# Earlier k and q loads, a step's shift of the value products, and VectorE's work re-dealt, in a kernel of attention and two MLPs

## The chip, the core and the metric

The kernel runs on one core of a Trainium2 chip. The metric is the device time of one execution in microseconds, as the median of several runs. TensorE does the matrix products, ScalarE (ACT) the activations, VectorE (DVE) the elementwise work; GpSimd (POOL) and SyncE (SP) mainly issue DMAs here, each into a DMA queue of its own.

## What is computed

```python
# attention: 4 batches, 12 heads, 448 positions, head size 64
scores = cap * tanh((q @ k^T / sqrt(64)) / cap)
attn   = softmax(scores)
x      = (attn @ v) as 1792 x 768
# first MLP: 768 -> 2048 -> 768
h = relu(x @ w_in);  x = (h * h) @ w_out
# second MLP: 768 -> 2048 -> 768
h = x @ w_in2;       out = (h * sigmoid(1.702 * h)) @ w_out2
```

## The kernel before

Attention comes first, the two MLPs after it. The MLPs' products are formed in Strassen's manner from seven products of sums; every fp32 operand is split into a rounded part and a rest (three matmuls for one product). The weights arrive in a form that has to be unpacked: a **chunk** of weights is loaded raw (`wraw`, on POOL's queue), ScalarE and VectorE unpack it (`join`: one `sx` on ACT, one `wy` on DVE), VectorE forms sums (`sums`: four operations), and POOL writes the result to DRAM scratch (`wsa`, `wsb`), from where SP loads it again for the products. There are 17 chunks for the first MLP; 11 of them are unpacked during attention, the rest in the first MLP's first phase.

Attention runs over 24 pairs of heads, two at a time: 12 **quads** of 4 heads. Each quad has four **steps** c = 0 to 3, one for each chunk of key positions; step s of the whole is 4n + c for quad n, and c = 3 is called TAIL. In a step TensorE makes the scores of both pairs (`sps`), ACT does tanh from PSUM and then exp, and TensorE multiplies earlier exponentials with `ones` (`vsps`, the softmax sums) and with v (`vxps`, `vyps`), as the table `PV` says: an entry (m, part, at) is for the quad m before the present one, its part s, x or y, and its key chunk. `take` copies the three sums out of PSUM, `invert` takes the reciprocal (DVE), `divide` multiplies and writes to DRAM scratch `xs` over POOL's queue; the entries (c, d) of `INVERT` and `DIVIDE` say in which step, and for the quad d before.

k and q of a pair are loaded by SP (`load_pair`), transposed on TensorE through the identity (`kps`, `qps`, or into the free half of a score bank, named `sps`), and split by DVE (`prep_k`, `prep_q`). A pair's k lies in one of two buffers `kz[p % 2]`, q in one of two of the pool `ld`. The steps in which they are transposed are not touched by the change: for quad m, pair 0's k in step 4m - 5, its q in step 4m - 4, pair 1's k and q in step 4m - 1. SP's queue is strictly in order: a load that waits for its buffer holds back all behind it.

`x_slice` (table `X_AT`) reads pieces of `xs` back and forms the first MLP's operands (`form`, and differences `sub`), three slices of five steps each: a read, then four times ACT and DVE work.

In each engine the instructions keep the order in which the program is written (`in_order`); `later` and `flush` put some DVE work at the next step's start. The loop over s at the end of the function issues attention, loads, weight slots (`ATT_WORK`, one `join` or `sums` each) and slices.

Of the kernel before, what the change touches and what calls it, by code (L numbers as in the profile page):

```python
# [677 lines left out]
def bounded_cap(ctx, tc, q, k, v, cap, w1, w2, w3, w4, out, over):  # L678

    nc = tc.nc  # L680
# [19 lines left out]
    Q_RAW = nc.gpsimd  # L700
# [9 lines left out]
    xf_p = att.enter_context(tc.tile_pool(name="xf", bufs=3, side="right"))  # L710
# [5 lines left out]
    ld = early.enter_context(tc.tile_pool(name="ld", bufs=2, side="right"))  # L716
# [25 lines left out]
    kz = [kz_p.tile([P, NCH, 2, D], F32, name=f"kz{i}") for i in range(2)]  # L742
# [33 lines left out]
    def load_pair(b, p):  # L776

        kt = kz[p % 2]
        qt = ld.tile([CP, NCH, 2, D], F32, tag="q", name="qt")
        queue = nc.scalar if (b, p) in quads[0] else Q_LOAD  # L780
        for j in range(2):
            Q_LOAD.dma_start(out=kt[:, :TAIL, j], in_=k[b, 2 * p + j, :MAIN].rearrange("(p c) d -> p c d", c=TAIL))
        for j, r in halves():
            Q_LOAD.dma_start(out=kt[r, TAIL, j], in_=k[b, 2 * p + j, MAIN:])
        for j in range(2):
            queue.dma_start(out=qt[:, :, j], in_=q[b, 2 * p + j].rearrange("(p c) d -> p c d", c=NCH))
        raw[b, p] = (qt, kt)
# [19 lines left out]
    def prep_k(b, p, ps=None):  # L807
        if ps is None:
            ps = transposed(raw[b, p][1], "kps")
        kk = prep[b, p, "k"] = qk_p.tile([P, 2, KW], F32R, tag="kk", name="kk")  # L810
        if (b, p) in quads[0]:
            a_.activation(kk[:, 0, :], ps, AF.Copy)
        else:
            v_.tensor_copy(kk[:, 0, :], ps)
        v_.tensor_tensor(kk[:, 1, :], ps, f32(kk[:, 0, :]), ALU.subtract)  # L815

    def prep_q(b, p, ps=None):
        if ps is None:
            ps = transposed(raw[b, p][0], "qps")
# [22 lines left out]
    def tanhs(b, p, c):  # L842
        if c == TAIL:
            e = et[b, p, c] = e_p.tile([P, 1, S], F32, tag="et", name="e", bufs=3)
# [27 lines left out]
    def take(n):  # L872

        last = wide("xo") if n == len(quads) - 1 else None
        for i, ps in enumerate(pvp[n]):
            t = x_p.tile([P, S], F32, tag=f"x{i}", name=f"x{i}") if last is None else last[:, i]
# [17 lines left out]
    def start_pair(b, p):  # L894
        prep_q(b, p, transposed(raw[b, p][0], "qps", ps_m.tile([P, 512], F32, tag="m", name="qps")))
        prep_k(b, p)

    def attn_step(s):
        n, c = divmod(s, NCH)
        ahead = quads[n + 1 : n + 3]  # L900
        for f, (at, d) in ((invert, INVERT), (divide, DIVIDE)):
            if c == at and 0 <= n - d < len(quads):
                f(n - d)
        now = quads[n] if n < len(quads) else ()
        more = []
        for i, x in enumerate(now):
# [3 lines left out]
            if c == TAIL and ahead:  # L910

                t = raw[ahead[0][1]][1 - i]
                more.append(transposed(t, "qps" if i else "kps", sc[(*x, c)][:, 1]))
# [6 lines left out]
        if c == TAIL and len(ahead) > 1:  # L920
            raw[ahead[1][0]] += (transposed(raw[ahead[1][0]][1], "kps"),)
# [5 lines left out]
        if c == 2 and 0 < n <= len(quads):  # L927
# [3 lines left out]
        if c == TAIL and len(ahead) > 1:  # L931
            prep_k(*ahead[1][0], raw[ahead[1][0]][2])

    def attn_loads(s):

        for d, f, i in ((6, load_pair, 0), (4, load_pair, 1), (1, load_v, 0), (0, load_v, 1)):
            m, at = divmod(s + d, NCH)
            if at == 0 and m < len(quads) and (m or f is load_v):
# [3 lines left out]
    def chunk_steps(l, kind, i):  # L942
# [77 lines left out]

    def weight_group(m):
# [11 lines left out]
    def weight_slot():  # L1033

        busy = False
        while work and (not busy or work[0][0].__name__.startswith("load")):
            f, *a = work.pop(0)
            if f.__name__ == "join":
# [112 lines left out]
    def x_slice(i, step):  # L1151
# [3 lines left out]
        def get(name, b, k0):  # L1155
            t = xin[name] = xf_p.tile([P, S], F32, tag=name, name="x" + name, bufs=1)
            Q_PUT.dma_start(out=t, in_=xs[b, k0 + i])

        def form(s, name):
# [4 lines left out]
            x = xin[name]  # L1164
# [3 lines left out]
        def sub(o, x, y):  # L1168
            o, x, y = xin[o], xin[x], xin[y]
# [227 lines left out]
    nc.gpsimd.memset(kz[1][:, TAIL], 0.0)  # L1397
    nc.scalar.dma_start(out=capt, in_=cap.rearrange("(o n) -> o n", o=1).to_broadcast([P, 1]))
    for x in quads[0]:
        load_pair(*x)  # L1400
# [4 lines left out]
    for s in range(-2, NCH * len(quads) + 3):  # L1405
        flush()
        if s >= 0:
            attn_step(s)
        attn_loads(s)
        flush()  # L1410
        if s == W_FIRST:
            weight_group(ATT_CHUNKS)
# [3 lines left out]
        if s in X_AT:  # L1416
            x_slice(*divmod(X_AT.index(s), 5))
# [75 lines left out]
E_BUFS = 10  # L1493
# [17 lines left out]
W_AT = 14  # L1511
W_AHEAD = 4
A_WORK = {(0, 0): 6, (0, 1): 6, (1, 0): 7}
# [46 lines left out]
```

## Time and profile before

| | |
|---|---|
| median of 3 runs | 1124.72 us (1120.51 to 1126.14) |
| the profiled execution's own time | 1117.81 us |
| its span, first to last instruction | 1116.0 us |
| TensorE busy in the span | 1053.9 us (94%) |
| VectorE, ScalarE, GpSimd busy | 826.2, 685.9, 278.6 us |
| moved by DMA | 228.36 MB |

The profiled execution lies 0.6% under the median of the runs. TensorE is busy for 94% of the span, so what it waits for, and the clock at which it runs, are read first.

### The profile page before, as it was taken

The numbers are of one execution on the slowest core, as the hardware profiler recorded it, in microseconds if no ns is written. First come the engines' busy times: TensorE is split into PE (matmuls) and PEld (weight loads), VectorE is DVE, ScalarE is ACT, GpSimd is POOL, SyncE is SP. The second block draws the span as 40 slices with busy tenths as digits, with TensorE's granted clock in tenths as the row PEclk, the third lists the DMA queues.
The fourth block names the chain that finished last, engine by engine and source line by source line (L and its number), as shares of the span: only waits on it lengthen the run. The fifth ranks groups of instructions, "written<-read, shape, count | busy, mean of one in ns | idle before, by whom it ended". The sixth has DMA issues, their size and how long they took to land.

```text
span 1116.0 us, 17045 instructions
## 1 busy us (share of the span) xinstructions
PE 1053.9 (94%) x5887; PEld 868.7 (78%) x5887; DVE 826.2 (74%) x1156; ACT 685.9 (61%) x1072; POOL 278.6 (25%) x418
## 2 busy tenths in 40 slices
PE   4998979799899999999999999999999999999997
PEld 2544434346799999989999998999799879998996
DVE  2487769768577987877689869778995885569854
ACT  2897868695567656466675655667555455565551
POOL 1042334321353013113210322343021520000133
PEclk9998989899999999999999999999999999999999
DMA  6399889854798467678864776898443743333433
GB/s 169 87 263 287 245 238 271 260 159 155 214 349 301 150 224 258 210 250 294 309 228 153 267 260 186 283 310 279 140 148 101 223 135 108 106 116 107 149 106 86
DMA packets 149616, 228.36 MB, mean 205 GB/s; under 512 B 65600, under 2 KB 102592, under 8 KB 149520
## 3 DMA queue, kind: packets, MB, share of 16 engines
q0 software_dynamic: 36768, 122.32, 33.9%
q1 hardware_dynamic: 110512, 104.29, 31.2%
q8 instruction: 48, 0.79, 0.3%
q10 hardware_dynamic: 2240, 0.57, 0.3%
q14 instruction: 48, 0.39, 0.1%
HBM read 166.53 MB, written 60.56 MB: 203 GB/s over the span
## 4 chain that ended last, share of the span: by engine, by line
PE 67%; DMA 10%; issue 9%; DVE 8%; ACT 3%; POOL 2%; SPq 0%; DVEq 0%; ACTq 0%; POOLq 0%
PE pa L1138 30%; PE pb L1138 28%; PE sps L834 3%; DMA kz<-in_k_dram 3%; DMA qt<-in_q_dram 3%; DVE form L1147 3%; DVE wl L1115 2%; DMA vz<-in_v_dram 2%; PE vxps L867 2%; PE vsps L867 2%; PE vyps L867 1%; DMA wf<-wsa 1%; ACT form L1146 1%; POOL wsb L994 1%; DVE qu L1348 1%
## 5 line engine op out<-in xcount | busy, mean ns | idle before, releaser
L1138 PE MATMUL pa<-form,wh 128*128 128x448 f32 x1536 | 441.0, 368 | 6.0 <-DVE form L1147 4.9
L1138 PE MATMUL pb<-form,wh 128*128 128x448 f32 x1152 | 330.3, 368 | 3.2 <-ACT qu L1345 2.3
L1138 PEld LDWEIGHTS pa<-form,wh 128*128 128x128 f32 x1536 | 288.9, 188 | 34.5 <-DVE form L1147 6.3
L1138 PE MATMUL pa<-form,wl 128*128 128x448 f32 x768 | 283.0, 368 | 4.9 <-DVE wl L1115 4.8
L1114 ACT ACTIVATE wh<-wf 128x384 fp32r<-128x384 f32 (+1 forms) x392 | 211.2, 560 | 75.8 <-DMA wf<-wsa 28.0
L1115 DVE TENSOR_TENSOR wl<-wf,wh 128x384 fp32r<-128x384 f32 (+1 forms) x392 | 225.9, 607 | 27.5 <-ACT wh L1114 27.0
L1138 PEld LDWEIGHTS pb<-form,wh 128*128 128x128 f32 x1152 | 217.2, 189 | 23.9 <-ACT qu L1345 3.1
L1138 PE MATMUL pb<-form,wl 128*128 128x448 f32 x576 | 211.4, 367 | 0.0
L1138 PEld LDWEIGHTS pa<-form,wl 128*128 128x128 f32 x768 | 144.8, 189 | 20.4 <-DVE wl L1115 7.8
L1328 POOL DMA_DIRECT2D out_dram<-o x92 | 57.7, 634 | 252.3 <-DVE o L1326 248.3
L1138 PEld LDWEIGHTS pb<-form,wl 128*128 128x128 f32 x576 | 108.4, 188 | 9.5
L1147 DVE TENSOR_TENSOR form<-g,form 128x1344 fp32r<-128x1344 f32 (+1 forms) x72 | 100.7, 1399 | 9.4 <-ACT form L1146 8.7
L847 ACT ACTIVATE e<-sps 128x896 f32<-128x896 f32 (+1 forms) x96 | 75.7, 822 | 47.7 <-PE sps L834 41.9
L979 DVE SCALAR_TENSOR_TENSOR wy<-wraw,sx 128x768 int32<-128x768 int32 (+1 forms) x68 | 61.8, 908 | 46.1 <-ACT sx L975 46.1
L1345 ACT ACTIVATE qu<-pb 128x448 f32<-128x448 f32 x88 | 47.5, 540 | 67.2 <-PE pb L1138 67.1
L834 PE MATMUL sps<-qq,kk 64*128 64x448 f32 (+1 forms) x504 | 81.0, 405 | 7.8 <-DVE kk L815 2.4
L1146 ACT ACTIVATE form<-g 128x1344 fp32r<-128x1344 f32 (+1 forms) x72 | 85.8, 1191 | 2.0 <-DVE g L1302 1.9
L834 PEld LDWEIGHTS sps<-qq,kk 64*128 64x128 f32 (+1 forms) x504 | 52.6, 198 | 43.5 <-ACT e L851 19.0
L851 ACT ACTIVATE e<-e,ecap 128x896 f32<-128x896 f32 (+1 forms) x96 | 85.7, 947 | 0.0
L975 ACT ACTIVATE sx<-wraw 128x768 f16<-128x768 bf16 (+1 forms) x68 | 69.5, 1022 | 0.0
L963 POOL DMA_DIRECT2D wraw<-in_moe_w_out_dram x72 | 53.2, 743 | 49.5 <-DVE wy L979 24.4
L1348 DVE SCALAR_TENSOR_TENSOR g<-pa,qu 128x448 f32<-128x448 f32 x64 | 39.8, 621 | 31.6 <-ACT qu L1345 16.8
(111 smaller groups left out, 1016.6 us busy)
## 6 DMA issues: line engine op xcount, KB each, us to landing
wf<-wsa SPq DMA_DIRECT2D x224, 192.0 KB, 4.0
wf<-wsb SPq DMA_DIRECT2D x168, 256.0 KB, 3.2
wraw<-in_moe_w_in_dram POOLq DMA_DIRECT2D x32, 766.5 KB, 8.3
wraw<-in_moe_w_out_dram POOLq DMA_DIRECT2D x48, 383.2 KB, 6.5
wsa<-wy POOLq DMA_DIRECT2D x32, 384.0 KB, 5.1
wsb<-wy POOLq DMA_DIRECT2D x24, 384.0 KB, 4.9
wsa<-ws POOLq DMA_DIRECT2D x16, 384.0 KB, 5.7
wraw<-in_moe_w_out_dram POOLq DMA_DIRECT2D x24, 255.5 KB, 5.6
```

The lines of the kernel that those rows point to most:

```text
L834: nc.tensor.matmul(ps[:, u, :S], x, y, start=all(t[0] != u for t in todo[:n]), stop=all(t[0] != u for t in todo[n + 1 :]),)
L847: a_.activation(e, chunk(c, sc.pop((b, p, c)))[:, :, :S], AF.Tanh)
L851: a_.activation(e, e, AF.Exp, scale=ecap)
L867: nc.tensor.matmul(ps[32 * i : 32 * i + 32, :S], x, t, start=c == 0, stop=c == TAIL, skip_group_check=True,)
L975: a_.activation(z, words(BF16)[:, :, :, 2], AF.Copy)
L979: v_.scalar_tensor_tensor(y[:, : 2 * n].bitcast(I32), words(I32)[:, :, :, 0], 13, sx[:, : 2 * n], ALU.logical_shift_right, ALU.bitwise_or,)
L1114: a_.activation(x, src, AF.Copy)
L1115: later.append(lambda: v_.tensor_tensor(y, src, f32(x), ALU.subtract))
L1138: nc.tensor.matmul(ps[:, :S], a[:, kk % 4, :], r, start=(s in (1, 5) and kk == 0 and n == 0), stop=(kk == ks - 1 and n == 2), skip_group_c ...
L1146: a_.activation(f[:, 0, :n, :], src, AF.Copy)
L1147: later.append(lambda: v_.tensor_tensor(f[:, 1, :n, :], src, f32(f[:, 0, :n, :]), ALU.subtract))
L1328: nc.gpsimd.dma_start(out=out[b * S : (b + 1) * S, m * P + 32 * j : m * P + 32 * j + 32].rearrange("(c p) d -> p c d", p=32), in_=o[32 * j ...
```

## The change

- k and q are loaded by functions of their own. k has four buffers (`KB`), by the pair's index, and q three (`QB`). `LOADS` requests pair 0's k in step 4m - 10 and its q in 4m - 8, pair 1's k in 4m - 8 and its q in 4m - 7 (before: pair 0 in 4m - 6, pair 1 in 4m - 4), and both pairs' v in 4m - 1 (before: 4m - 1 and 4m). The loop begins at s = -6 so that the first requests are made.
- Products with v are one step sooner (`PV`), and so are `take` and the last reads of the exponentials; these have 8 and 2 buffers, before 10 and 3.
- The reciprocal moves to c = 2, the division to c = 0; weight slots are at TAIL, and two at c = 0; the x slices lie in steps 25 to 48 (before 27 to 44), with two buffers each.
- Ten chunks are unpacked in attention and seven in the first MLP, whose slots begin at its 10th product (before: the 14th). The eleventh chunk is a small one (two thirds of the others).
- Before the first raw weights are loaded, POOL copies one element of a TAIL exponential of quad 0 into `ones` and restores it.
- `raw_queue`, `held`, `RAW_AT` stay without effect while `RAWQ` is POOL's queue.

```diff
-    kz = [... for i in range(2)]
+    kz = [... for i in range(KB)]
...
-    def load_pair(b, p):
-        kt = kz[p % 2]
-        qt = ld.tile([CP, NCH, 2, D], F32, tag="q", name="qt")
...
+    def load_k(b, p):
+        kt = raw[b, p, "k"] = kz[pairs.index((b, p)) % KB]
...
+    def load_q(b, p):
+        qt = raw[b, p, "q"] = ld.tile([CP, NCH, 2, D], F32, tag="q", name="qt")
...
-        for d, f, i in ((6, load_pair, 0), (4, load_pair, 1), (1, load_v, 0), (0, load_v, 1)):
+        for d, f, i in LOADS:
+            f = {"k": load_k, "q": load_q, "v": load_v}[f]
             m, at = divmod(s + d, NCH)
...
         if s == W_FIRST:
+            nc.gpsimd.tensor_copy(ones[:1, 0, :1], et[(*pairs[0], TAIL)][:1, 0, :1])
+            nc.gpsimd.memset(ones[:1, 0, :1], 1.0)
             weight_group(ATT_CHUNKS)
...
-E_BUFS = 10
+E_BUFS = 8
 PV = (
-    ((1, 1, 0), (1, 2, 0), (1, 1, 1)),
     ((1, 2, 1), (1, 0, 2), (1, 1, 2)),
     ((1, 2, 2), (1, 0, 3), (1, 1, 3), (1, 2, 3)),
     ((0, 0, 0), (0, 0, 1)),
+    ((0, 1, 0), (0, 2, 0), (0, 1, 1)),
 )
-INVERT = (0, 2)
-DIVIDE = (1, 2)
-ATT_CHUNKS = 11
+TAKE = 1
+INVERT = (2, 1)
+DIVIDE = (0, 2)
+ATT_CHUNKS = 10
-ATT_WORK = tuple(sorted([4 * n + i for n in range(1, 11) for i in (3, 5, 6)] + [12, 20, 28]))
-X_AT = tuple(s + 6 * i for i in range(3) for s in (27, 29, 30, 31, 32))
+ATT_WORK = tuple(sorted([4 * n + i for n in range(1, 11) for i in (3, 4, 4)]))
+X_AT = (25, 27, 29, 31, 33, 29, 35, 37, 39, 41, 36, 43, 45, 47, 48)
-W_AT = 14
+W_AT = 10
+LOADS = ((8, "q", 0), (8, "k", 1), (7, "q", 1), (10, "k", 0), (1, "v", 0), (1, "v", 1))
+KB = 4
+QB = 3
-A_WORK = {(0, 0): 6, (0, 1): 6, (1, 0): 7}
+A_WORK = {(0, 0): 17 - ATT_CHUNKS, (0, 1): 6, (1, 0): 7}
```

On SP, in the first quads, the queue of before is this (`kz_115`, `kz_116` are the k buffers, `vz` the v buffers):

```order
L782 DMA kz_115<-in_k_dram 128x3x64 x2
L784 DMA kz_115<-in_k_dram 64x64 x2
L786 DMA qt<-in_q_dram 112x4x64 x2
L792 DMA vz_117<-in_v_dram 128x2x192
L797 DMA vz_117<-in_v_dram 64x64 x2
L782 DMA kz_116<-in_k_dram 128x3x64 x2
L784 DMA kz_116<-in_k_dram 64x64 x2
L786 DMA qt<-in_q_dram 112x4x64 x2
L792 DMA vz_118<-in_v_dram 128x2x192
L797 DMA vz_118<-in_v_dram 64x64 x2
```

and of the change, from the first v load on, this:

```order
L792 DMA vz_119<-in_v_dram 128x2x192
L797 DMA vz_119<-in_v_dram 64x64 x2
L792 DMA vz_120<-in_v_dram 128x2x192
L797 DMA vz_120<-in_v_dram 64x64 x2
L787 DMA qt<-in_q_dram 112x4x64 x2
L779 DMA kz_116<-in_k_dram 128x3x64 x2
L781 DMA kz_116<-in_k_dram 64x64 x2
L787 DMA qt<-in_q_dram 112x4x64 x2
L779 DMA kz_117<-in_k_dram 128x3x64 x2
L781 DMA kz_117<-in_k_dram 64x64 x2
```

The number of loads is the same; a k load now goes into a buffer that was last read two quads earlier, and both v loads of a quad stand together, ahead of the q and k of the quad after the next.

On TensorE, around TAIL of quad 1, the program of before has this:

```order
L834 MATMUL sps<-qq,kk 128x448 x3
L804 MATMUL sps<-ident,kz_116 128x128 x4
L834 MATMUL sps<-qq,kk 128x448 x3
L804 MATMUL sps<-ident,qt 128x112 x4
L804 MATMUL kps<-ident,kz_115 128x128 x4
L867 MATMUL vsps<-e,ones 32x448 x8
L834 MATMUL sps<-qq,kk 128x448 x12
```

and that of the change this:

```order
L867 MATMUL vsps<-e,ones 32x448 x8
L834 MATMUL sps<-qq,kk 128x448 x3
L804 MATMUL sps<-ident,kz_116 128x128 x4
L834 MATMUL sps<-qq,kk 128x448 x3
L804 MATMUL sps<-ident,qt 128x112 x4
L804 MATMUL kps<-ident,kz_117 128x128 x4
L867 MATMUL vxps<-e,vz_121 32x448 x2
L867 MATMUL vxps<-e,vz_122 32x448 x2
L867 MATMUL vyps<-e,vz_121 32x448 x2
L867 MATMUL vyps<-e,vz_122 32x448 x2
L867 MATMUL vxps<-e,vz_121 32x448 x2
L867 MATMUL vxps<-e,vz_122 32x448 x2
```

The softmax sums (`vsps`) moved ahead of TAIL's scores, and three groups with v fill the place between the transposes and the next quad's scores (`sps` x12, which follow). Each row `x2` is twice that many matmuls in the profile.

On POOL, before the first raw weights, the change has two instructions that wait for attention, where before the loads followed the memsets at once:

```order
L1411 MEMSET vz_121 128x128
L1411 MEMSET vz_122 128x128
L1426 COPY ones<-e 1x1
L1427 MEMSET ones 1x1
L964 DMA wraw<-in_moe_w_in_dram 128x6x1022 x3
```

So the three raw loads come after quad 0's TAIL exponential and after the `vsps` of step 4 on TensorE.

## Rows read from the trace of the kernel before

**Rows 1.** Waits of TensorE from 0 to 300 us: total us, times, longest us.

```profile
PE qps L804 <- DMA qt<-in_q_dram: 16.3, 3, 6.7
PE kps L804 <- DMA kz<-in_k_dram: 15.6, 3, 6.3
PE sps L834 <- DVE kk L815: 2.4, 2, 1.4
PE sps L834 <- DVE qq L822: 2.1, 5, 0.4
```

**Rows 2.** Busy time by stretch: three quads, quads 0 to 11, first MLP.

```profile
core 0: us, PE busy (x) PEld busy (x) DVE busy (x) ACT busy (x) POOL busy (x), PEclk, DMA share, GB/s
51.52:68.55 17.03, 17.03 (x156) 8.58 (x155) 13.25 (x18) 15.16 (x20) 4.37 (x6) 1.00 0.76 184
68.55:86.25 17.70, 17.29 (x156) 8.53 (x155) 15.36 (x22) 16.40 (x21) 7.43 (x12) 1.00 1.04 309
86.25:109.28 23.03, 17.88 (x156) 8.83 (x155) 16.23 (x23) 17.59 (x23) 7.41 (x10) 0.91 0.97 284
...
34.49:252.93 218.44, 194.81 (x1676) 94.53 (x1675) 158.41 (x221) 171.78 (x223) 69.00 (x97) 0.95 0.81 231
...
300.00:450.00 150.00, 150.00 (x739) 138.71 (x740) 124.12 (x178) 100.11 (x164) 44.13 (x64) 1.00 0.77 255
```

**Rows 3.** TensorE in order of time: start us, us, instruction, idle before.

```profile
8.57 1.49 PE L834 MATMUL sps<-qq,kk 64*128 64x448 f32 x6 [0.69 <-ACT kk L812]
16.71 1.01 PE L804 MATMUL qps<-ident,qt 112*128 112x112 f32 x4 [6.66 <-DMA qt<-in_q_dram]
...
30.46 1.49 PE L834 MATMUL sps<-qq,kk 128*128 128x448 f32 x3 [1.80 <-ACT e L847]
...
51.52 1.71 PE L867 MATMUL vsps<-e,ones 128*32 128x448 f32 x16
...
85.71 0.60 PE L804 MATMUL kps<-ident,kz 128*128 128x128 f32 x4
...
108.26 1.09 PE L804 MATMUL kps<-ident,kz 128*128 128x128 f32 x4 [5.15 <-DMA kz<-in_k_dram]
109.28 2.98 PE L867 MATMUL vsps<-e,ones 128*32 128x448 f32 x16
...
199.75 0.57 PE L804 MATMUL qps<-ident,qt 112*128 112x112 f32 x4 [3.55 <-DMA qt<-in_q_dram]
```

**Rows 4.** Busy time by stretch, columns as in Rows 2, behind a wait.

```profile
110.00:111.00 1.00, 1.00 (x12) 0.40 (x8) 0.97 (x3) 0.00 (x0) 0.00 (x0) 0.50 1.04 279
```

**Rows 5.** The chain that ended last: start us, us, what; two loads.

```profile
4.76 11.90 DMA qt<-in_q_dram
...
97.00 11.16 DMA kz<-in_k_dram
```

**Rows 6.** DMA queues from 0 to 20 us: packets, MB, share of 16 engines.

```profile
q0 software_dynamic: 528, 2.35, 38.5%
```

**Rows 7.** The page's DMA issues: count, KB each, median us to landing.

```profile
wraw<-in_moe_w_in_dram POOLq DMA_DIRECT2D x32, 766.5 KB, 8.3
...
wsa<-wy POOLq DMA_DIRECT2D x32, 384.0 KB, 5.1
...
qt<-in_q_dram SPq DMA_DIRECT2D x44, 112.0 KB, 5.4
```

**Rows 8.** DMA queues from 68 to 217 us (q0 POOL's, q1 SP's).

```profile
q0 software_dynamic: 9451, 29.21, 60.5%
q1 hardware_dynamic: 32488, 9.65, 29.8%
```

**Rows 9.** SP's DMA queue from 127 to 152 us.

```profile
q1 hardware_dynamic: 3789, 1.12, 20.0%
```

**Rows 10.** Transfers that write or read `xs`.

```profile
DMA to landing us min/median/max: 4.9/7.9/11.4
```

**Rows 11.** Transfers from `xs` into `xt`.

```profile
DMA to landing us min/median/max: 6.6/8.7/9.8
```

More of the change, by code (lines that the diff above doesn't have):

```diff
@@ L784, in load_pair @@
             Q_LOAD.dma_start(out=kt[r, TAIL, j], in_=k[b, 2 * p + j, MAIN:])
+    def load_q(b, p):
+        qt = raw[b, p, "q"] = ld.tile([CP, NCH, 2, D], F32, tag="q", name="qt")
+        queue = nc.scalar if (b, p) in quads[0] else Q_LOAD
         for j in range(2):
             queue.dma_start(out=qt[:, :, j], in_=q[b, 2 * p + j].rearrange("(p c) d -> p c d", c=NCH))
-        raw[b, p] = (qt, kt)
     def load_v(b, p):
@@ L808, in prep_k @@
         if ps is None:
-            ps = transposed(raw[b, p][1], "kps")
+            ps = transposed(raw[b, p, "k"], "kps")
         kk = prep[b, p, "k"] = qk_p.tile([P, 2, KW], F32R, tag="kk", name="kk")
@@ L818, in prep_q @@
         if ps is None:
-            ps = transposed(raw[b, p][0], "qps")
+            ps = transposed(raw[b, p, "q"], "qps")
         qq = prep[b, p, "q"] = qk_p.tile([P, 2, S], F32R, tag="qq", name="qq")
@@ L875, in take @@
         for i, ps in enumerate(pvp[n]):
-            t = x_p.tile([P, S], F32, tag=f"x{i}", name=f"x{i}") if last is None else last[:, i]
+            t = x_p.tile([P, S], F32, tag=f"x{i}", name=f"x{i}", bufs=2 if i else 1) if last is None else last[:, i]
             if i:
@@ L894, in start_pair @@
     def start_pair(b, p):
-        prep_q(b, p, transposed(raw[b, p][0], "qps", ps_m.tile([P, 512], F32, tag="m", name="qps")))
+        prep_q(b, p, transposed(raw[b, p, "q"], "qps", ps_m.tile([P, 512], F32, tag="m", name="qps")))
         prep_k(b, p)
@@ L901, in attn_step @@
         for f, (at, d) in ((invert, INVERT), (divide, DIVIDE)):
-            if c == at and 0 <= n - d < len(quads):
+            if c == at and 0 <= n - d < len(quads) - 1:
                 f(n - d)
@@ L910, in attn_step @@
             if c == TAIL and ahead:
-                t = raw[ahead[0][1]][1 - i]
+                t = raw[(*ahead[0][1], "q" if i else "k")]
                 more.append(transposed(t, "qps" if i else "kps", sc[(*x, c)][:, 1]))
@@ L920, in attn_step @@
         if c == TAIL and len(ahead) > 1:
-            raw[ahead[1][0]] += (transposed(raw[ahead[1][0]][1], "kps"),)
+            kps = transposed(raw[(*ahead[1][0], "k")], "kps")
         for m, part, at in PV[c]:
@@ L926, in attn_step @@
             exps(*x, c)
-        if c == 2 and 0 < n <= len(quads):
+        if c == TAKE and 0 < n <= len(quads):
             take(n - 1)
@@ L931, in attn_step @@
         if c == TAIL and len(ahead) > 1:
-            prep_k(*ahead[1][0], raw[ahead[1][0]][2])
+            prep_k(*ahead[1][0], kps)
     def attn_loads(s):
-        for d, f, i in ((6, load_pair, 0), (4, load_pair, 1), (1, load_v, 0), (0, load_v, 1)):
+        for d, f, i in LOADS:
+            f = {"k": load_k, "q": load_q, "v": load_v}[f]
             m, at = divmod(s + d, NCH)
-            if at == 0 and m < len(quads) and (m or f is load_v):
+            if at == 0 and 0 <= m < len(quads) and (m or f == load_v):
                 f(*quads[m][i])
@@ L1019, in bounded_cap @@
     work = []
+    raw_queue = [RAWQ(nc)]
+    held = []
     def weight_group(m):
@@ L1037, in weight_slot @@
             f, *a = work.pop(0)
-            if f.__name__ == "join":
+            if f.__name__ == "load" and raw_queue[0] is nc.sync:
+                held.append((step_now[0] + 2, f, a))
+            elif f.__name__ == "join":
                 f(*a)
@@ L1396, in bounded_cap @@
     nc.vector.memset(kz[0][:, TAIL], 0.0)
-    nc.gpsimd.memset(kz[1][:, TAIL], 0.0)
+    for t in kz[1:]:
+        nc.gpsimd.memset(t[:, TAIL], 0.0)
     nc.scalar.dma_start(out=capt, in_=cap.rearrange("(o n) -> o n", o=1).to_broadcast([P, 1]))
     for x in quads[0]:
-        load_pair(*x)
+        load_k(*x)
+        load_q(*x)
     emit_const()
@@ L1404, in bounded_cap @@
     start_pair(*pairs[0])
-    for s in range(-2, NCH * len(quads) + 3):
+    step_now = [0]
+    for s in range(-6, NCH * len(quads) + 3):
         flush()
+        step_now[0] = s
         if s >= 0:
```

29 lines of the change are left out of this document (17 added, 12 removed).

## The prediction

> **What bounds the kernel now.** I read the busy times by stretch first [rows 2]. In 150 us of the first MLP TensorE has no idle time (150.00 us busy), so next to nothing is to be had there, except by disturbing it. In attention it is different. A quad without waits at full clock takes 17.03 us, all of it TensorE. From the `vsps` of quad 0 to those of quad 11 eleven such spans would be 11 x 17.03 = 187.3 us; the trace has 218.4, that is 31.1 us more. Next the waits [rows 1]: TensorE stood 15.6 us for k and 16.3 us for q. Of the three waits for q one lies between the quads (3.55 us) and two at the start: the second pair's (6.66 us [rows 3]) and the first q's, the remaining 6.1 us, before which nothing can run. So 15.6 + 3.6 = 19.2 us lie between the quads. Another 4.5 us are waits for VectorE's `kk` and `qq`. The rest, 31.1 - 19.2 - 4.5 = 7.4 us, is slow clock: behind a wait the same 16 `vsps` take 2.98 us instead of 1.71 [rows 3], and the granted clock there is 0.50, the 1.2 GHz level, although TensorE is at work again for the whole stretch [rows 4]. So late loads cost 26.6 us between the quads.
>
> Why they are late: the chain shows one k load issued at 97.00 that took 11.16 us [rows 5]; TensorE needed it at 103.1 and got it at 108.2, with 5.15 us of wait [rows 3]. Its buffer had been free since the transposes at 85.71 [rows 3], the TAIL before, but SP's queue, in order, came to it only at 97. With 21 us of lead the 11 us would not hurt.
>
> VectorE and ACT are next in line: in a quad of 17.70 us, 17.29 of them TensorE's, they were busy 15.36 and 16.40 us [rows 2]. So TensorE stays the floor at 17.03, but by 0.6 us over ACT.
>
> **The change, part by part.** Gains are counted against the profiled execution's own 1117.81 us.
>
> *Start.* The second pair's q took 11.90 us [rows 5], while POOL's raw weight loads moved 2.35 MB of the first 20 us, 38.5% of all engines' time, 7.7 us [rows 6]. The change holds them until step 4. The first pair's scores end at 8.57 + 1.49 = 10.1 [rows 3], so the wait of 6.66 us can vanish. Against that, more k and q of quad 1 may be issued at once, about 670 KB: at 217 GB/s (below) up to 3 us. **+6.0** (3.6 to 6.6). The gate itself: POOL's two tiny writes stand between the `vsps` of steps 4 and 5, where TensorE has 12 score matmuls and more to do; nothing. The loads then fall into quads 0 and 1, still before their first `join` in step 7.
>
> *k and q between the quads.* With four and three buffers the tightest load is pair 0's q: its buffer is read last in step 4m - 9, it is needed in 4m - 4, five steps or 21 us. Pair 0's k is asked for in 4m - 10 and needed in 4m - 5, pair 1's k and q get six steps or more. v is needed one step sooner (4m + 3) and is asked for in 4m - 1, its buffers free in 4m - 3: four steps, 17 us, and nothing else is queued ahead of it that waits longer than it does. All exceed the 11 to 12 us of the slowest two loads in the chain [rows 5]. SP issues as many loads as before. **+26.6** if no wait is left (0 to 26.6); what is left of it is priced under the DMA engines.
>
> *VectorE's waits.* `vsps` x16 (1.71 us [rows 3]) leaves the place between the transposes and the next quad's scores, and three groups of eight matmuls come in; a group is half of those 16 in number, so 3 x 0.86 = 2.6 us, and the chain from the transposes to `kk` and `qq` gets 0.9 us more. The longest `qq` wait is 0.4 us, the longest `kk` wait 1.4 [rows 1]. The reciprocal now stands at c = 2, ahead of the transposes, and the weight sums leave the step before TAIL. **+3.5** of 4.5 (0 to 4.5).
>
> *Quad 0.* While TensorE waits 1.80 us for ACT [rows 3] it can do the 16 `vsps` that come sooner; but they wait for ACT as well. **+0.8** (0 to 1.6).
>
> *x slices.* The division of quad 4 comes in step 24, the first slice's read in step 25, its first use on ACT at the end of step 27. The reads wait for the writes. A step is 17.03 / 4 = 4.26 us; the writes are issued about one step after step 24 begins and land 7.9 us later [rows 10], three reads are issued and land 8.7 us later [rows 11]: 4.3 + 7.9 + 1 + 8.7 = 22 us, where ACT arrives after four steps, 17 us. ACT would wait some 5 us, and TensorE behind it less, since the scores already made keep it going for part of that. **-3** (0 with the fastest landings, 4.9 and 6.6; -9.5 with the slowest, 11.4 and 9.8). The other slices have six steps or more between read and use: nothing.
>
> *The DMA engines.* From 68 to 217 us (seven quads) the two queues filled 60.5% + 29.8% = 90.3% of 149 us, 134.6 us [rows 8]. Of before's weight slots 24 fall there, eight chunks; now seven. A chunk reads 2 x 766.5 KB and writes 384 KB three times and half of that once [rows 7], 2.95 MB; at POOL's 29.21 MB in 90.1 us, 324 GB/s, that is 9.1 us. So 125.5 us of transfers are to go into 7 x 17.03 = 119.2 us: a share of 1.05. The fullest quad of before reached 1.04, with 0.4 us of waiting, the next 0.97 [rows 2]. At 1.04 the engines would add 2 us over the ten quads with chunks, at 0.97 about 14, at the mean of 0.90 about 20 in the seven. I take a third of this: **-6** (0 to -20), nearer to the full quad, because the deeper buffers keep SP's queue supplied where it was held up before.
>
> *The MLP.* The small chunk costs there what it saves in attention; VectorE and ACT have 26 and 50 us to spare in 150 [rows 2]. Its first raw load comes about four products earlier. If ACT stood a whole landing of 8.3 us [rows 7] for it, the weights split four products ahead (9 matmuls of 150/739 us, 1.83 us each, so 7.3 us) would nearly cover it. **0** (-3 to 0). The smaller numbers of exponential buffers cost nothing: each is read last one or two steps before it is written again. If ACT falls a step behind, that cover is gone.
>
> Sum: 6.0 + 26.6 + 3.5 + 0.8 - 3 - 6 = 27.9 us, so 1090 us for the profiled execution. The median of the runs lies 6.9 us above that execution, so on the median: 1124.7 - 28 = **1096 us** or so.
>
> **The rivals.**
>
> A. *The DMA engines become the bound.* For it: 1.05 is asked, 0.90 was the mean. Against it: that mean contains times in which SP's queue was held up by buffers. Then -20 in place of -6: 1124.7 - 14 = 1111 us.
>
> B. *Loads asked for early are not served early.* SP's queue got 1.12 MB through from 127 to 152 us [rows 9], 45 GB/s, beside POOL's large transfers; a quad needs 9.65 / 7 = 1.38 MB, 31 us at that rate. Then the 26.6 us stay, and the other terms (with nothing for the engines) give 7: 1117 us. Against it: over seven quads it did carry 9.65 MB, in 29.8% of the engines' time (217 GB/s), so the engines had room for it at other times. The Trainium skill (DMA: Bandwidth & Descriptors, section Queues, rings and completion order) says that each DMA engine takes turns between the queues with work, a packet at a time. By that rule a queue of small packets falls behind one of large ones, which is this rival; the low rate from 127 to 152 us agrees with it, without showing that it is the cause.
>
> C. *Slower: ACT stands behind the raw weights.* `join` is in order on ACT, and its load has at the shortest about 20 us (one quad and one step, less the unpacking). If SP's earlier loads push it past that, each of 20 joins waits. ACT has 17.03 - 16.40 = 0.6 us to spare in a quad [rows 2]; with 3 us for each join TensorE loses 2 x 3 - 0.6 = 5.4 us in each of ten quads, 54 us: 1124.7 - 28 + 54 = 1151 us. It is slower than before by over 0.5% when a join waits more than about 2 us, a landing of some 22 us. Against it: 8.3 us is the median now [rows 7], in the same crowd.
>
> **How the numbers follow.** My forecast, 1096 us with a range of its own of 1086 (every term at its good end: 39 us) to 1106, has a chance of 0.68; A 0.16; B 0.09; C 0.07. The 80% range reaches into A: 1084 to 1113 us. About 0.5% (5.6 us) is what a measurement of this kernel tells from no change. Faster by more: the forecast, A and a part of B, 0.86; within it the rest of B, 0.07; slower C, 0.07.
>
> **What would show it.** In the new trace: the wait for the second pair's q near 10 us instead of 16.7; no `kps` or `qps` wait for a DMA after quad 0; `vsps` groups of 1.71 us throughout; quads of 17.0 to 17.7 us; attention over near 234 instead of 262. One ACT wait for `xt` of a few us. A would show as several DMA waits with a share over 0.95; B as waits as long as now; C as ACT waiting for `wraw`. A first MLP phase with new TensorE idle time would prove the zero for the MLP wrong.

## The result, and the profile after

| | before | after |
|---|---|---|
| median of four runs each | 1123.38 us | 1092.09 us (1090.30 to 1094.28) |
| profiled execution, its own time | 1117.81 us | 1090.30 us |
| its span | 1116.0 us | 1087.7 us |
| first output product of the MLP | 262.08 us | 234.13 us |
| from there to the end | 853.9 us | 853.6 us |

The ratio of the times is 0.9723, with a 95% interval of 0.9690 to 0.9755: the change is faster by 2.8%. 1096 us were forecast, and 27.9 us less for the profiled execution; its span is 28.3 us shorter. The last two rows put all of it into attention.

The page of the changed kernel, span and busy times:

```profile
span 1087.7 us, 17044 instructions
...
PE 1050.3 (97%) x5887; PEld 865.8 (80%) x5887; DVE 825.1 (76%) x1156; ACT 685.3 (63%) x1072; POOL 279.9 (26%) x422
```

Waits of TensorE from 0 to 300 us, against [rows 1]:

```profile
PE qps L804 <- DMA qt<-in_q_dram: 7.0, 2, 6.1
PE vxps L867 <- DMA vz<-in_v_dram: 6.9, 3, 4.4
PE qps L804 <- issue: 1.6, 1, 1.6
PE sps L834 <- ACT kk L812: 1.4, 2, 0.7
```

The waits for k and for VectorE are gone, that for q has fallen from 16.3 to 7.0 us, and most of the 7.0 is the very first q, for which nothing can be done here. In their place stands a wait that the kernel before did not have: 6.9 us for v. TensorE in order of time, the start and the two longer waits for v, against [rows 3]:

```profile
10.02 1.01 PE L804 MATMUL qps<-ident,qt 112*128 112x112 f32 x4
...
16.65 0.98 PE L804 MATMUL qps<-ident,qt 112*128 112x112 f32 x4 [1.56 <-issue]
...
99.58 0.73 PE L867 MATMUL vxps<-e,vz 128*32 128x448 f32 x2 [2.31 <-DMA vz<-in_v_dram]
...
157.97 0.96 PE L867 MATMUL vxps<-e,vz 128*32 128x448 f32 x2 [4.36 <-DMA vz<-in_v_dram]
```

The second pair's q is transposed at 10.02 us, without a wait; it was 16.71 us. Busy times by stretch, against [rows 2]: quads 0 to 11, three quads (the second and third hold the two waits above), the first MLP.

```profile
core 0: us, PE busy (x) PEld busy (x) DVE busy (x) ACT busy (x) POOL busy (x), PEclk, DMA share, GB/s
22.06:223.42 201.36, 193.20 (x1688) 94.82 (x1687) 153.99 (x212) 169.21 (x220) 66.62 (x95) 0.98 0.87 251
56.55:73.58 17.03, 17.03 (x156) 8.59 (x154) 14.09 (x20) 15.08 (x20) 5.88 (x8) 1.00 0.95 273
91.79:113.98 22.19, 19.74 (x156) 9.06 (x154) 14.10 (x20) 15.06 (x20) 5.51 (x8) 0.92 0.84 241
148.35:172.31 23.96, 19.59 (x154) 9.00 (x154) 17.11 (x25) 16.82 (x24) 8.72 (x14) 0.93 0.93 265
300.00:450.00 150.00, 150.00 (x728) 136.25 (x727) 124.80 (x165) 92.11 (x142) 34.80 (x52) 1.00 0.71 236
```

A quad whose loads come in time takes the 17.03 us of TensorE's work at a DMA share of 0.95. In the two quads with a late v TensorE is not only idle for 2.4 and 4.4 us; its work also takes 2.7 and 2.6 us longer, at a granted clock of 0.92 and 0.93. The first MLP is unchanged.

### The profile page after: what moved, and what is told of

Same layout as the page of the kernel before. It is cut to its first block, busy times and chain, and to the rows that moved or that the text cites. A ratio compares the mean times of both kernels' runs of the same rounds, so it can differ in the third digit from the quotient of the medians.

```text
span 1087.7 us, 17044 instructions
## 1 busy us (share of the span) xinstructions
PE 1050.3 (97%) x5887; PEld 865.8 (80%) x5887; DVE 825.1 (76%) x1156; ACT 685.3 (63%) x1072; POOL 279.9 (26%) x422
## 4 chain that ended last, share of the span: by engine, by line
PE 63%; issue 14%; DVE 10%; DMA 7%; POOL 4%; ACT 2%; ACTq 0%; DVEq 0%; POOLq 0%
PE pa L1144 30%; PE pb L1144 29%; DMA xs<-x 4%; DVE form L1153 3%; DVE wl L1121 2%; PE sps L834 1%; POOL wsa L995 1%; DMA wf<-wsa 1%; DMA out_dram<-o 1%; DMA xl<-ys 1%; POOL wraw L964 1%; POOL xs L892 1%; DVE g L1269 1%; DVE g L1354 1%; ACT form L1152 1%
## 5 line engine op out<-in xcount | busy, mean ns | idle before, releaser
L1121 DVE TENSOR_TENSOR wl<-wf,wh 128x384 fp32r<-128x384 f32 (+1 forms) x392 | 225.4, 606 | 18.3 <-ACT wh L1120 17.6
L834 PE MATMUL sps<-qq,kk 64*128 64x448 f32 (+1 forms) x504 | 77.4, 396 | 1.4 <-ACT kk L812 1.4
L834 PEld LDWEIGHTS sps<-qq,kk 64*128 64x128 f32 (+1 forms) x504 | 51.5, 193 | 33.8 <-ACT e L847 10.3
L1354 DVE SCALAR_TENSOR_TENSOR g<-pa,qu 128x448 f32<-128x448 f32 x64 | 39.8, 622 | 33.2 <-PE pa L1144 17.1
```

What stands on the lines that cost most here:

```text
L834: nc.tensor.matmul(ps[:, u, :S], x, y, start=all(t[0] != u for t in todo[:n]), stop=all(t[0] != u for t in todo[n + 1 :]),)
L1121: later.append(lambda: v_.tensor_tensor(y, src, f32(x), ALU.subtract))
```

## The experiments

Each run lists its median, the ratio to the kernel before on the same chip with its 95% interval, and two readings of its profiled execution: what TensorE waited for k, q and v after the first q (in the kernel before 25.8 us, of it 6.7 for the second pair's q; in the changed kernel 7.8), and when the first output product came. Executions of one kernel differ by some us (those of the kernel before spread over 1112 to 1136 us), so a single profile places a wait, and the ratios carry the size. "Change without the last keys" and "change, half of the raw weights" leave out loads, so their results are not the reference's.

| kernel | median us | ratio, interval | k, q, v waits | first output product |
|---|---|---|---|---|
| change, v asked for two steps sooner | 1100.25 | 0.9769, 0.9727 to 0.9810 | 16.5 | 243.50 |
| change without POOL's gate | 1095.90 | 0.9737, 0.9691 to 0.9784 | 13.6 | 238.18 |
| change with the loads of before | 1098.19 | 0.9760, 0.9707 to 0.9814 | 18.4 | 245.73 |
| change with the products of before | 1097.90 | 0.9754, 0.9688 to 0.9820 | 11.2 | 239.15 |
| change, half of the raw weights | 1100.34 | 0.9798, 0.9727 to 0.9870 | 15.4 | 245.38 |
| before, weight slots of the change | 1111.69 | 0.9900, 0.9826 to 0.9974 | 21.5 | 256.99 |
| before, gate alone | 1123.72 | 0.9981, 0.9937 to 1.0025 | 21.1 | 261.85 |
| before, loads alone | 1116.93 | 0.9946, 0.9908 to 0.9985 | 19.0 | 260.18 |
| change without the last keys of k and v | 1076.21 | 0.9592, 0.9515 to 0.9670 | 0 | 221.51 |
| change, k and q in one DMA a pair | 1081.67 | 0.9643, 0.9566 to 0.9720 | 3.7 | 226.88 |
| change, v on POOL's queue | 1077.26 | 0.9606, 0.9522 to 0.9689 | 0 | 219.74 |
| before, k and q in one DMA a pair | 1111.38 | 0.9888, 0.9832 to 0.9945 | 19.4 | 255.49 |

Two theories stood at first. **Theory one**: the order of SP's queue decides which load is late; v stands behind the early q and k, so v asked for sooner is in time. **Theory two**: the DMA engines are full in the quads with weight chunks, and something is always late.

**v sooner.**

```diff
-LOADS = ((8, "q", 0), (8, "k", 1), (7, "q", 1), (10, "k", 0), (1, "v", 0), (1, "v", 1))
+LOADS = ((3, "v", 0), (3, "v", 1), (8, "q", 0), (8, "k", 1), (7, "q", 1), (10, "k", 0))
```

> Both v loads of a quad are asked for in step 4m - 3, when their buffers are free, instead of 4m - 1; all else as in the changed kernel. Theory one (v is late because it stands behind the q and k of later quads in SP's queue): the 6.9 us of waits for v and the slow clock behind them, some 5 us, go: 1092 - 12 = 1080 us, and no new wait over 2 us. Theory two (the DMA engines are full, something is always late): v is in time, but k or q of pair 0 is late in the same two places, 1089 to 1095 us.

TensorE's waits in that kernel, same view as above:

```profile
PE kps L804 <- DMA kz<-in_k_dram: 10.1, 2, 6.5
PE sps L804 <- DMA qt<-in_q_dram: 6.4, 2, 5.2
PE qps L804 <- DMA qt<-in_q_dram: 6.2, 1, 6.2
```

No wait for v is left, and 16.5 us for k and q have come. Theory one falls in its plain form: the lateness moves to whatever the order puts last. The late k and q are what theory two foresaw, but the median of 1100.25 us is above what either expected.

**Without the gate.**

```diff
-            nc.gpsimd.tensor_copy(ones[:1, 0, :1], et[(*pairs[0], TAIL)][:1, 0, :1])
-            nc.gpsimd.memset(ones[:1, 0, :1], 1.0)
```

> POOL's two instructions ahead of the raw weights are taken out of the changed kernel. Theory one: the second pair's q is late again at the start, TensorE waits about 6.6 us there, and nothing else changes: 1098 to 1099 us. Theory two (the engines are full later): 2.35 MB, 7.7 us of transfers, leave quads 0 and 1 and move into the start, so that the waits for v shrink, and the whole loses only 0 to 3 us: 1092 to 1095 us.

The second pair's q is late again by 6.8 us, but the first output product comes only 4.05 us later than with the gate. The median, 1095.90 us, lies between the two expectations, and its interval contains both.

**The loads of before.**

```diff
-LOADS = ((8, "q", 0), (8, "k", 1), (7, "q", 1), (10, "k", 0), (1, "v", 0), (1, "v", 1))
-KB = 4
-QB = 3
+LOADS = ((6, "k", 0), (6, "q", 0), (4, "k", 1), (4, "q", 1), (1, "v", 0), (0, "v", 1))
+KB = 2
+QB = 2
```

> The changed kernel with k and q in two buffers each and all loads asked for in the steps of before; the gate, the products with v a step sooner and VectorE's order stay. Theory one: the late k and q come back, 20 to 27 us less the 12 us that late v costs now at most: 1105 to 1118 us, with waits for k and q of 10 us or more between the quads. Theory two (the gate and the evened-out weight slots did most of it): less than 6 us slower, under 1098 us.

11.6 us of attention are lost, less than half of the change's 27.95; a single transposition waits 8.7 us. The waits, 18.4 us, are as theory one had them; the time, 1098.19 us, is 7 us under its range and at the edge of theory two's.

**The products of before** (`PV`, `TAKE`, `INVERT`, `DIVIDE`, `X_AT`).

```diff
-    ((0, 1, 0), (0, 2, 0), (0, 1, 1)),
+    ((1, 1, 0), (1, 2, 0), (1, 1, 1)),
...
-TAKE = 1
-INVERT = (2, 1)
-DIVIDE = (0, 2)
+TAKE = 2
+INVERT = (0, 2)
+DIVIDE = (1, 2)
...
-X_AT = (25, 27, 29, 31, 33, 29, 35, 37, 39, 41, 36, 43, 45, 47, 48)
+X_AT = tuple(s + 6 * i for i in range(3) for s in (27, 29, 30, 31, 32))
```

> The changed kernel with the products with v, the take, the reciprocal, the division and the x slices in the steps of before. Theory one: v has a step, 4.3 us, more, so waits for v (6.9 us and the slow clock) nearly go; VectorE's waits come back with 3.5 to 4.5 us, quad 0's 0.8 us too: net 1083 to 1088 us. Rival: the shift was worth more than that on VectorE, whose work now piles up before TAIL again together with the weight slots: kk and qq waits over 8 us, 1095 us or more.

v, needed a step later, is in time; instead one q is late by 11.2 us, and 5.0 us of attention are lost. The time is the rival's, its cause is not: the one wait for `qq` is 0.4 us.

**Half of the raw weights.**

```diff
         def load(u):
+            if u and light[0]:
+                return
...
-            t = st.pop(("r", u))[:, : 2 * n]
+            t = st.pop(("r", u), None)
+            t = st["t0"] if t is None else t
+            st["t0"] = t
+            t = t[:, : 2 * n]
```

> The changed kernel, in which in attention the second of each chunk's two raw loads is left out (766.5 KB less for each of ten chunks, at 324 GB/s some 24 us of transfers, 2.4 us in each quad); the second unpacking reads the first half again, so half of the weights unpacked in attention are copies of the other half. The engines' work is the same. Theory two (the DMA engines are full in the quads with chunks, and whichever of k, q and v is behind is late): the seven quads from 68 us on then ask for a share of about 0.9 in place of 1.05; TensorE's waits for k, q and v fall from 13.9 us to under 9 (the start's 6.1 stay), the first output product comes at 222 to 228 us in place of 234, median 1079 to 1086 us. Theory one (what is late is decided by the order of SP's queue, not by the load): v of quad 4 is still asked for behind q and k and is late, the waits stay at 12 to 14 us, the first output product at 232 to 235, median 1089 to 1094 us.

The waits for v in that kernel:

```profile
PE vxps L867 <- DMA vz<-in_v_dram: 15.4, 6, 5.2
```

And its busy times from 22 to 230 us, columns as above:

```profile
22.00:230.00 208.00, 192.65 (x1642) 93.30 (x1634) 149.85 (x205) 164.32 (x212) 54.82 (x80) 0.97 0.73 203
```

In the same stretch the changed kernel has a share of 0.88 and 252 GB/s. With engines that are idle for more than a quarter of the time, TensorE waits for v more than twice as long. For the changed kernel theory two falls; theory one foresaw waits that stay, but not waits that double, and what doubled them stays open.

**The parts alone, on the kernel before.** The weight slots:

```diff
-ATT_CHUNKS = 11
+ATT_CHUNKS = 10
...
-ATT_WORK = tuple(sorted([4 * n + i for n in range(1, 11) for i in (3, 5, 6)] + [12, 20, 28]))
+ATT_WORK = tuple(sorted([4 * n + i for n in range(1, 11) for i in (3, 4, 4)]))
...
-W_AT = 14
+W_AT = 10
...
-A_WORK = {(0, 0): 6, (0, 1): 6, (1, 0): 7}
+A_WORK = {(0, 0): 17 - ATT_CHUNKS, (0, 1): 6, (1, 0): 7}
```

> The kernel before with only the weight slots of the change: ten chunks in attention, evenly placed, seven in the first MLP. Theory two: one chunk less is 9.1 us less to transfer in quads that ask for more than the engines give; the waits for k and q between the quads (19.2 us) and the slow clock behind them lose 5 to 10 us, median 1114 to 1119 us. Theory one: k and q are late because SP's queue is held up by their buffers; they stay late, 0 to 2 us are gained, median 1122 to 1125 us.

The gate (the two lines above, added):

> The kernel before with only POOL's gate ahead of the first raw weights. The wait of 6.66 us for the second pair's q falls to under 1 us, if the gate alone brings the start's gain: the first sums of quad 0 come 6 to 7 us sooner. Theory two: the held raw weights fall into quads 0 and 1, where the engines have room, so nearly all of it stays to the end, median 1116 to 1119 us. Theory one says the same here; the rival is that the transfers held back are only moved on, and are paid for by a later wait: median 1121 to 1125 us.

The loads (`load_k`, `load_q`, `LOADS`, `KB = 4`, `QB = 3` and the buffers' numbers):

> The kernel before with only the changed loads: k in four buffers, q in three, asked for a quad ahead, without the gate, with the eleven chunks, the weight slots, the products and the slices of before. By the prediction's terms 26.6 - 6 = 20.6 us are gained, and less the engines' share of one more chunk some 15 to 20: median 1105 to 1110 us. Theory two: the engines still have the eleven chunks to carry and something stays late; 5 to 12 us are gained (undoing the loads cost about 11.6 us of attention), median 1111 to 1118 us, with waits for k, q or v of 10 to 15 us between the quads in place of 19.2.

In the kernel with the gate alone, the first sums on TensorE in order of time:

```profile
28.02 1.71 PE L867 MATMUL vsps<-e,ones 128*32 128x448 f32 x16
```

And what TensorE waited for until the output products:

```profile
PE kps L804 <- DMA kz<-in_k_dram: 19.4, 5, 8.3
PE qps L804 <- DMA qt<-in_q_dram: 7.7, 2, 6.0
```

And its busy times from quad 0 to quad 11, columns as above:

```profile
28.02:252.69 224.67, 198.91 (x1675) 95.44 (x1674) 158.21 (x221) 171.75 (x223) 71.90 (x102) 0.92 0.83 237
```

Its quad 0 is 6.47 us ahead of the kernel before (28.02 against 34.49), and its first output product 0.23 us. Between the quads k and q are waited for 1.9 us longer (21.1 us in place of 19.2), and TensorE's work takes 4.1 us longer (198.91 us in place of 194.81, at a granted clock of 0.92 in place of 0.95): together they take back the rest. The rival written beside that run is what came. The slots alone bring 1.0%, the loads 0.5%, the gate nothing that can be told from none; in the profiles 5.1, 1.9 and 0.2 us, together 7.2 of the change's 27.95. The shift of the products was not run alone. The loads alone came out in theory two's range (1116.93 us, and 12.9 us of waits between the quads, where the prediction's terms gave 1105 to 1110 us), and the slots alone brought more than theory two asked for, with 15.1 us of waits for k and q between the quads in place of 19.2. So in the kernel before, what POOL transfers may have a part in the late loads. A stage earlier in time helps little while the loads behind it come no sooner.

**What all of these have in common** is SP. Its queue in the changed kernel in order of time (start us, us, and x1 or x2 for one or two DMAs), at the start and where v of quad 4 is issued:

```profile
0.74 1.35 SPq L779 DMA_DIRECT2D kz<-in_k_dram  x2
2.14 1.31 SPq L781 DMA_DIRECT2D kz<-in_k_dram  x2
...
82.59 1.31 SPq L779 DMA_DIRECT2D kz<-in_k_dram  x2
83.94 1.28 SPq L781 DMA_DIRECT2D kz<-in_k_dram  x2
85.32 0.78 SPq L792 DMA_DIRECT2D vz<-in_v_dram  x1
86.20 3.94 SPq L797 DMA_DIRECT2D vz<-in_v_dram  x2
90.20 0.58 SPq L792 DMA_DIRECT2D vz<-in_v_dram  x1
90.87 2.35 SPq L797 DMA_DIRECT2D vz<-in_v_dram  x2
```

SP goes from one DMA to the next with few pauses. In the first 20 us the 30 DMAs take 18.6 us, 0.62 each; from 45 to 220 us 160 take 155.7 us, 0.97 each (what SP stands for inside these times, the profile does not name reliably). A quad has 18, so some 17.5 us, and lasts 17.03. v of quad 4 is due in step 15, which begins at about 75 us, and is issued from 85.3 to 93.2; TensorE wanted it at 97.3. In the kernel with half of the raw weights it is 152 DMAs in 153.2 us, 1.01 each: no better. So **theory three**: it is the number of DMAs that SP issues that is full. And its rival, **theory four**: it is their packets (the pieces, of 256 bytes in k, q and the tails of v, that a DMA is cut into), 4352 in a quad, which get through at some 215 to 230 in 1 us.

**Without the last 64 keys of k and v** (the loads at L781 and L797 are left out):

```diff
-        for j, r in halves():
-            Q_LOAD.dma_start(out=kt[r, TAIL, j], in_=k[b, 2 * p + j, MAIN:])
...
-        for j, r in halves():
-            Q_LOAD.dma_start(out=vt[r, 2 * TAIL + j], in_=v[b, 2 * p + j, MAIN:])
```

> The changed kernel without the loads of the last 64 keys of k and v (these keys count as zero, so the result isn't the reference's). This takes 8 of the 18 DMAs that SP issues for a quad, but only 512 of their 4352 packets (12%) and 6% of their bytes. Theory three (SP's issuing is what is full: an issue takes 0.62 us in the first 20 us and 0.9 to 1.1 from 45 us on, 18 of them a quad's whole 17 us, so that SP is always behind whatever the order): with 10 issues a quad, 10 to 12 us, TensorE waits for no k, q or v after the start; the first output product comes at 219 to 224 us in place of 234.1, median 1077 to 1083 us. Theory four (SP's packets get through at some 215 to 230 in 1 us beside POOL's transfers, and 4352 take longer than a quad): 3840 packets still take 17 to 18 us; the waits after the start fall from 7.8 us to 3 to 6, first output product at 228 to 232, median 1086 to 1090 us.

TensorE's longest waits in that kernel:

```profile
PE qps L800 <- DMA qt<-in_q_dram: 6.5, 1, 6.5
PE qps L800 <- issue: 1.6, 1, 1.6
PE sps L830 <- ACT kk L808: 1.4, 2, 0.7
```

And v of quad 4 in SP's queue, in order of time (L790 is the v load there):

```profile
74.44 1.72 SPq L790 DMA_DIRECT2D vz<-in_v_dram  x1
```

Nothing after the first q is late; v of quad 4 is issued 10.9 us sooner, when it is due. The times are theory three's; but the packets fell too, to 3840 in a quad, which at 228 in 1 us (below) take 16.8 us and would also be in time.

**One DMA for both heads of a pair.**

```diff
-        for j in range(2):
-            Q_LOAD.dma_start(out=kt[:, :TAIL, j], in_=k[b, 2 * p + j, :MAIN].rearrange("(p c) d -> p c d", c=TAIL))
+        h = slice(2 * p, 2 * p + 2)
+        Q_LOAD.dma_start(out=kt[:, :TAIL], in_=k[b, h, :MAIN].rearrange("h (p c) d -> p c h d", c=TAIL))
...
-        for j in range(2):
-            queue.dma_start(out=qt[:, :, j], in_=q[b, 2 * p + j].rearrange("(p c) d -> p c d", c=NCH))
+        h = slice(2 * p, 2 * p + 2)
+        queue.dma_start(out=qt, in_=q[b, h].rearrange("h (p c) d -> p c h d", c=NCH))
```

> The changed kernel in which one DMA loads the k of both heads of a pair, and one the q: 14 issues on SP in a quad in place of 18, with the same packets and bytes and the whole result. Theory three, if one issue costs what it did (0.9 to 1.0 us): 13 to 14 us of issues in 17.03, the waits after the start fall under 2 us, first output product at 220 to 226 us, median 1078 to 1085 us. Theory four: the packets are the same, so nothing changes by more than the waits vary, first output product at 231 to 240, median 1090 to 1098 us; the issues are then longer, so that SP is as full as it was.

```profile
PE qps L804 <- DMA qt<-in_q_dram: 7.1, 2, 6.3
PE vxps L867 <- DMA vz<-in_v_dram: 2.9, 1, 2.9
```

The waits of that kernel: of 7.8 us after the first q 3.7 are left, and the first output product comes 7.25 us sooner. Theory four expected 231 to 240 us and no change; theory three asked for waits under 2 us and missed that a little. The times are nearer to theory three, though the interval of the ratio (0.9566 to 0.9720) still touches the changed kernel's (0.9690 to 0.9755). The pace of SP's queue is theory four's. The v loads of quads 3 and 9 are issued, in the changed kernel,

```profile
66.80 0.53 SPq L792 DMA_DIRECT2D vz<-in_v_dram  x1
...
181.52 0.53 SPq L792 DMA_DIRECT2D vz<-in_v_dram  x1
```

and with one DMA for both heads,

```profile
60.59 0.74 SPq L792 DMA_DIRECT2D vz<-in_v_dram  x1
...
175.22 0.53 SPq L792 DMA_DIRECT2D vz<-in_v_dram  x1
```

Six quads take 114.7 us with 18 DMAs each and 114.6 us with 14, 19.1 us a quad both times (one profile of each): between these quads four DMAs less saved SP nothing, and v is again issued up to 9 us after it is due (quad 5: 101.9 us, where its step begins at 92.5). An issue now takes longer (from 45 to 220 us 122 DMAs in 159.9 us, 1.31 each), the sign that was written down for theory four, and 4352 packets in 19.1 us are 228 in 1 us, its rate. What this kernel gains is a head start, 6.2 us at quad 3: SP is through the first quads' loads sooner, at the time when an issue costs 0.62 us whatever its packets.

**v on POOL's queue** (the first quad's v stays on SP's).

```diff
+        queue = Q_LOAD if (b, p) in quads[0] else nc.gpsimd
         h = slice(2 * p, 2 * p + 2)
-        Q_LOAD.dma_start(
+        queue.dma_start(
...
-            Q_LOAD.dma_start(out=vt[r, 2 * TAIL + j], in_=v[b, 2 * p + j, MAIN:])
+            queue.dma_start(out=vt[r, 2 * TAIL + j], in_=v[b, 2 * p + j, MAIN:])
```

> The changed kernel with the loads of v on POOL's queue: SP keeps 12 issues and 3584 packets a quad. Theory three: 11 to 12 us of issues, no k or q is late; theory four: 3584 packets at 215 to 230 in 1 us take 15.6 to 16.7 us, just in time as well. Both expect no wait for k or q after the start, and first output product at 219 to 226 us, median 1077 to 1085 us, unless v is late in its new place: it stands behind POOL's weight writes, which wait for VectorE, and then waits for v of 5 us and more are left, median 1090 or more.

TensorE's longest waits in that kernel:

```profile
PE qps L805 <- DMA qt<-in_q_dram: 6.2, 1, 6.2
PE qps L805 <- issue: 1.6, 1, 1.6
```

And its busy times from quad 0 to quad 11, and in one quad, columns as above:

```profile
22.13:209.03 186.90, 186.90 (x1689) 93.74 (x1687) 154.02 (x212) 169.34 (x220) 102.94 (x155) 1.00 0.93 266
90.77:107.80 17.03, 17.03 (x157) 8.59 (x155) 14.09 (x20) 15.09 (x20) 10.41 (x17) 1.00 0.97 278
```

Eleven quads without one idle moment of TensorE, at full clock, with the same bytes and a DMA share of 0.97 in a quad that waits for nothing. This version beats both kernels: its first output product comes 14.4 us before the changed kernel's, its median is 1077.26 us. It doesn't tell theory three from theory four, which both expected it: SP is rid of six DMAs and of 768 packets.

The Trainium skill (DMA: Bandwidth & Descriptors, section Issuing engines are not separate DMA queues) says that issuing from several engines saves only the time that it takes to initiate the DMAs, usually small beside the DMA itself. One issue is small beside its DMA here too: 0.97 us on SP in the mean, beside a median of 7.0 us from the issue of a q load to its landing (45 to 205 us). Yet moving six of 18 DMAs to another queue took every wait away; whether what it saved is SP's time for issuing or the pace at which SP's queue is served, the runs do not separate.

**One DMA for both heads, on the kernel before.** The same two edits, in `load_pair`.

> The kernel before, nothing of the change in it, with one DMA for the k of both heads of a pair and one for the q: SP issues 14 DMAs a quad in place of 18, with the same packets and bytes, into the same two buffers, asked for in the same steps. Theory three (the number of DMAs on SP's queue is what made k and q late in the kernel before as well): the waits for k and q between the quads fall from 19.2 us to 4 to 10, first output product at 242 to 252 us in place of 262.1, median 1104 to 1114 us. The rival, as the prediction has it (k and q are late because SP's queue is held up by buffers that are too few, and stands behind v's): the buffers and the queue's order are the same, so the waits stay at 15 to 20 us, first output product at 257 to 262, median 1119 to 1124 us.

```profile
PE kps L803 <- DMA kz<-in_k_dram: 19.4, 5, 6.9
PE qps L803 <- DMA qt<-in_q_dram: 6.3, 1, 6.3
```

Of the 19.4 us, 2.17 are at the start and 17.2 between the quads, where there were 19.2. Here the rival holds for the waits, and theory three doesn't reach back to the kernel before: with two buffers of k, fewer DMAs do not bring k sooner. (With four, in the kernel with the loads alone, TensorE waited 3.3 us for k.) The kernel is 1.1% faster all the same: the median, 1111.38 us, is in theory three's range, and the first output product lies between the two ranges, 6.6 us sooner; 3.6 us of these are a sooner quad 0 (its sums at 30.88 in place of 34.49).

## Why the prediction was right, and where not

The waits of TensorE up to the first output product were 41.4 us (the four groups of [rows 1] and 5.0 us for ACT and its own sequencer) and are 17.1. That is 24.3 us; the other 3.6 of the 27.95 are work that went faster, at the full clock.

- *The start*, +6.0 forecast: the waits for the first q's fell from 12.7 to 6.1 us, 6.6. Right; but only in this company: alone, the gate brings nothing.
- *VectorE's waits*, +3.5: both are gone, 4.5. Right, at the good end.
- *Quad 0*, +0.8: the 2.0 us for ACT are gone, and 0.2 us for VectorE have come. That is 1.8, a little over the good end of 1.6.
- *x slices*, -3: ACT waits once for `xt`, 2.0 us where 5 were estimated (2.7 in the kernel before), and TensorE has no wait for it. The term was 3 us too large. ACT's wait:

```profile
ACT form L1171 <- DMA xt<-xs: 2.0, 1, 2.0
```

- *k and q between the quads*, +26.6. The reading of the kernel before agrees with the runs: its loads were late because SP's queue came to them late, and halving the number of k's and q's main DMAs into the same buffers left 17.2 of 19.2 us. The waits for k are gone, and 0.95 us for q is left. But the term holds only in company: the loads alone left 12.9 us of waits for k, q and v between the quads and brought 0.5%. **The step that failed is the sentence on v**: that four steps are enough because "nothing else is queued ahead of it that waits longer than it does". Each load ahead of it costs SP's time, and v, whose lead is the shortest, is what SP reaches 10 us late (85.3 us, where step 15 begins at about 75).
- *The DMA engines*, -6: the size came out, 7.8 us of waits for v and q, but by luck, since the cause was another. A share of 1.05 was asked and taken as the bound; with v on POOL's queue the same bytes go through at 0.97 without a wait, and with fewer bytes in the kernel with half the raw weights the waits grew. The quads with a late v have shares of 0.84 and 0.93, under the 0.95 that the prediction named as the sign of full engines. "SP issues as many loads as before" was taken for a cost of nothing, where SP's queue was the scarce one.
- *The slow clock*, 7.4 of the 26.6, was to vanish with the waits. Between the quads TensorE's work took 194.8 us and takes 193.2; where nothing waits it takes 186.9. So 1.6 of 7.9 were gained: late v brought the 1.2 GHz level back. Together the terms for k and q, the slices and the engines, forecast at 26.6 - 3 - 6 = 17.6 us, came to 11.4 of waits and 1.6 of clock, 13.0; the total still fits because the start, VectorE and quad 0, with 2.0 us of clock outside the eleven quads (what is left of the 3.6), gave 14.9 where 10.3 were forecast. That these two errors cancel is luck.
- *The MLP*, 0: 853.9 and 853.6 us. Right.

Of the signs, the second pair's q at 10 us and attention over at 234 us came; quads of 17.0 to 17.7 us did not, where v was late (22.2 and 24.0 us), and one wait for q was left. Of the rivals, A's price (20 us in place of 6) did not come, and its mechanism fell. B came in part: v was late because it was issued late, and SP's queue got its packets through at one pace, 228 in 1 us, whether in 18 DMAs a quad or in 14, and a slow queue is what B is about. C did not come: ACT has no wait for `wraw` in attention.

That SP's queue is what makes v late in the changed kernel is shown: with v on another queue, or without the tails, no load is late. That the number of its DMAs is what fills it is not shown, and the equal pace with 14 and with 18 speaks against it. Two things in the traces bear on what an issue waits for. SP's DMAs take eight semaphores in turn, never more than eight are between issue and landing, and of the changed kernel's 17 pauses over 0.3 us from 45 to 220 us 16, in all 14.4 us, end as the DMA eight before lands. And an issue is long where many packets of its queue are still unmoved: a DMA of 64 pieces takes 0.52 us in the mean with fewer than 400 unmoved and 1.17 us with more than 1200; with one DMA for both heads it is 0.55 and 2.32 us. Open are what sets the pace of 228 packets in 1 us beside POOL's transfers, and why v is later still with half of the raw weights.

## What to carry over

Before costing moved loads at nothing, read how long a queue takes for one period of the loop: here SP's took 19.1 us for the loads of a quad of 17.03. The time of one issue is no constant to multiply by: with 14 DMAs in place of 18, and the same packets, it grew from 0.97 to 1.31 us, and the period stayed. When a load comes late, read when it was issued before asking how long it took; if its queue is behind all the time, asking sooner only chose which load was late here, and less in the queue, or another queue, cured it. Parts tried alone need not add up: here slots, loads and gate bring 7.2 us alone, one by one, against 27.95 for all together with the shift of the products.

## What the runs showed of the hardware

- One DMA issue on SP took 0.60 to 0.68 us in the first 16 us, alike for 64 (L781), 384 (L779) or 448 (`qt`) pieces of 256 bytes; later, beside POOL's transfers, 0.97 us in the mean, and 1.01 with half of the raw weights (all queues moved 203 GB/s there, in place of 252).
- The 16 DMA engines ran at a share of 0.97 and 278 GB/s for a quad, with the packets of 256 bytes of k and q among them, while every load came in time: a share near 1 was not yet a sign of late loads.
- Two DMAs made into one, with the same packets, saved time only in the first quads: later SP's queue took 19.1 us a quad with 14 DMAs as with 18, 228 packets in 1 us, and the issues became longer (1.31 us in place of 0.97).
- In every trace here SP's queue had at most eight DMAs between issue and landing: each waits for the semaphore of the one eight before it.
